# The last 96 rows of a second-layer contraction as 32-row array tiles, with five accumulation banks for that layer

One core of one Trainium2 chip (trn2). The metric is the device time of one execution in microseconds (us), the slowest core's; here there is only one core.

## The reference

Two branches over the same 2048 tokens of 512 features, mixed by a gate. Branch A is a linear attention with 32 heads; branch B is two dense layers with a ReLU between, 512 to 1376 to 512. Cut to what matters:

```python
g = sigmoid((x * gate_w).sum(-1, keepdims=True))
# A: softmax feature maps of q and k, then per head
kv  = einsum("bhsf,bhsd->bhfd", phi_k, v)
num = einsum("bhqf,bhfd->bhqd", phi_q, kv);  den = ...
a   = (num / den) @ wo
# B
h = maximum(x @ w1, 0)          # 2048 x 1376
b = h @ w2                      # contraction 1376 = 10 * 128 + 96
return g * a + (1 - g) * b
```

The second layer of B contracts over 1376 rows: ten full blocks of 128 and a rest of 96. The change is about that rest.

## The kernel before

All engines get their instructions from one plan with explicit events. The last stage (from about 87 us) works on 16 token tiles of 128 tokens. For each it runs four things: the numerators and denominators of the attention (`nd`, eight small matmuls, then a reciprocal and a product on VectorE, DVE below, then a transpose by DMA), the second layer (`finB`, eleven matmuls), the projection (`finA`, four matmuls, then a scaled copy on ScalarE, ACT below) and the combination (`comb`, one DVE instruction and the output copy).

```python
def nd(m):
    b0 = 2 * (m % 2)                                  # two pairs of PSUM banks
    ...                                               # 8 matmuls into banks b0, b0 + 1
    ...                                               # DVE: RDEN = 1/den; OTM = num * RDEN
    free[b0] = free[b0 + 1] = [f"om{m}"]
    p.dma("sp", lambda e: e.dma_start_transpose(
        out=OT[:, :, m * P:(m + 1) * P], in_=OTM[:, ob, :]), f"to{ob}", after=[f"om{m}"], ev=f"to{m}")

def finB(m, bank, cs=slice(0, 512), tag=""):
    for kt in range(KT):                              # KT = 11
        M = P if kt < KU else NR                      # the last one has NR = 96 rows
        p.op("pe", lambda e, kt=kt, M=M: e.matmul(
            PS[:, bank, 0:n], HT[0:M, kt, m * P:(m + 1) * P], W2[0:M, kt, cs],
            start=(kt == 0), stop=(kt == KT - 1)), ...)

def finA(m, bank):                                    # waits for the transpose to{m}
    for t in range(NDT):
        p.op("pe", lambda e, t=t: e.matmul(
            PS[:, bank, :], OT[:, t, m * P:(m + 1) * P], WO[:, t, :],
            start=(t == 0), stop=(t == NDT - 1)),
            after=(["wo", f"to{m}"] + free[bank] if t == 0 else ()), ...)
    ...                                               # ACT: TFA = GT * bank

FB = (4, 5, 7)                                        # banks of the second layer
for m in range(NT):
    if m > 1 and m + 3 < NT:
        nd(m + 3)                                     # three tiles ahead
    if m + 1 < NT - 1:
        finB(m + 1, FB[(m + 1) % 3])
    ...                                               # the first tiles: nd(2), nd(3), nd(4)
    finA(m, (6, 2, 0)[max(m - NT + 3, 0)])
    if m < NT - 1:
        comb(m)
...                                                   # tile 15: second layer in two cuts
```

The softmax here doesn't subtract the row's maximum and nothing guards it: scores larger than these inputs give would overflow.

Of the kernel before, what the change touches and what calls it, by code (L numbers as in the profile page):

```python
# [5 lines left out]
ACT = mybir.ActivationFunctionType  # L6
# [3 lines left out]
BF16 = mybir.dt.bfloat16  # L10
# [58 lines left out]
def bass_gated_mix__linear_kernel_hedgehog__dense_activation_relu__prompt_kernel(  # L69
# [13 lines left out]
    S, D = x2.shape  # L83
    H = A_w_phi.shape[0]
    DH = A_w_phi.shape[1]
    DFF = B_w1.shape[1]
    P = 128
    NT = S // P
    NDT = D // P
    NCH = S // 512  # L90
    KT = (DFF + P - 1) // P
# [10 lines left out]
    KU = KT - 1  # L102
    NR = DFF - KU * P

    with ExitStack() as es:
        E = es.enter_context
# [12 lines left out]
        PHQ = E(nc.sbuf_tensor("PHQ", [P, NG, S], BF16))  # L119
        KVNZ = E(nc.sbuf_tensor("KVNZ", [P, NG, 68], BF16))  # L120
        OT = E(nc.sbuf_tensor("OT", [P, NDT, S], BF16))
        HR = E(nc.sbuf_tensor("HR", [P, 2, 4, P], BF16))
        ROWI = E(nc.sbuf_tensor("ROWI", [P, P], I32))
        COLI = E(nc.sbuf_tensor("COLI", [P, P], I32))
        ONE = E(nc.sbuf_tensor("ONE", [P, 1], BF16))
# [11 lines left out]
        GT = E(nc.sbuf_tensor("GT", [P, NT], FP32))  # L137
        OMG = E(nc.sbuf_tensor("OMG", [P, NT], FP32))
        RDEN = E(nc.sbuf_tensor("RDEN", [P, 2, H], FP32))
        TFA = E(nc.sbuf_tensor("TFA", [P, 2, D], BF16))  # L140
        PS = E(nc.psum_tensor("PS", [P, 8, 512], FP32))

        XS = OT[:, 0, :].rearrange("p (j d) -> p j d", j=4)
        WQKT = PHQ[:, :, S - 512:S]
        OTM = WQK[:, 0, 0:3 * D].rearrange("p (a b) -> p a b", a=3)
        OSB = WQK[:, 1, 0:3 * D].rearrange("p (a b) -> p a b", a=3)
        EPS = 8 * 512
# [4 lines left out]
        free = {b: [] for b in range(8)}  # L152
# [126 lines left out]
        def rest(c):  # L279
            bank = nextbank()  # L280
            for i in range(4):
                for s in range(NDT):
                    t0 = c * 512 + i * P
                    p.op("pe", lambda e, i=i, s=s, t0=t0: e.matmul(  # L284
                        PS[:, bank, i * P:i * P + NR + 1], XT[:, s, t0:t0 + P], W1[:, s, KU * P:DFF + 1],
                        start=(i == 0 and s == 0), stop=(s == NDT - 1), skip_group_check=True),
                        after=(xready(c) + w1all + ["gw"] + free[bank] if i == 0 and s == 0 else ()),
                        ev=(f"h{c}_r" if i == 3 and s == NDT - 1 else None))
            src = PS[:, bank, :].rearrange("p (i n) -> p i n", i=4)
            b = c % 2  # L290
            p.op("act", lambda e: e.activation(HR[:, b, :, 0:NR], src[:, :, 0:NR], ACT.Relu),
                 after=[f"h{c}_r"] + ([f"hr{c - 2}"] if c >= 2 else []), ev=f"rr{c}")
            p.op("act", lambda e: e.activation(
                EG[:, 4 * c:4 * c + 4].unsqueeze(2), src[:, :, NR:NR + 1], ACT.Exp, scale=-1.0), ev=f"eg{c}")
            free[bank] = [f"eg{c}"]
            p.dma("sp", lambda e: e.dma_start_transpose(
                out=HT[:, KU, c * 512:(c + 1) * 512].rearrange("p (i t) -> p i t", i=4),
                in_=HR[:, b, :, :].rearrange("p i n -> p (i n)")), f"hr{c}", after=[f"rr{c}", f"hz{b}"], ev=f"hr{c}")

        def pre(i):  # L300
            which, dt = i // 4, i % 4
# [162 lines left out]
                 after=["g"], ev="gt")  # L464

        def nd(m):
            b0 = 2 * (m % 2)
            after = [f"tq{m}", "kvz0"] + free[b0] + free[b0 + 1]
            for g in range(NG):
                p.op("pe", lambda e, g=g: e.matmul(  # L470
                    PS[:, b0 + g // 4, (g % 4) * GW:(g % 4) * GW + 68],
                    PHQ[:, g, m * P:(m + 1) * P], KVNZ[:, g, :], start=True, stop=True),
                    after=(after if g == 0 else ["kvz1"] if g == 4 else ()), ev=(f"nd{m}" if g == NG - 1 else None))
            r = m % 2
            ob = m % 3
            p.op("dve", lambda e: e.reciprocal(
                RDEN[:, r, :].rearrange("p (g h) -> p g h", g=NG),
                bass.AP(tensor=PS, offset=b0 * 512 + 64, ap=[[EPS, P], [GW, NG], [1, HG]])),
                after=[f"nd{m}"], ev=f"rd{m}")
            p.op("dve", lambda e: e.tensor_tensor(  # L480
                OTM[:, ob, :].rearrange("p (g h d) -> p g h d", g=NG, h=HG),
                bass.AP(tensor=PS, offset=b0 * 512, ap=[[EPS, P], [GW, NG], [DH, HG], [1, DH]]),
                bass.AP(tensor=RDEN, offset=r * H, ap=[[2 * H, P], [HG, NG], [1, HG], [0, DH]]), ALU.mult),
                after=[f"rd{m}"] + ([f"to{m - 3}"] if m >= 3 else []), ev=f"om{m}")
# [3 lines that stand above are left out]

        fbank = {}

        def finB(m, bank, cs=slice(0, 512), tag=""):
            n = cs.stop - cs.start
            for kt in range(KT):
                M = P if kt < KU else NR
                p.op("pe", lambda e, kt=kt, M=M: e.matmul(  # L495
                    PS[:, bank, 0:n], HT[0:M, kt, m * P:(m + 1) * P], W2[0:M, kt, cs],
                    start=(kt == 0), stop=(kt == KT - 1)),
                    after=(["w2", f"hr{m // 4}", f"rl{m // 4}_{KU - 1}"] + free[bank] if kt == 0 else ()),
                    ev=(f"fb{m}{tag}" if kt == KT - 1 else None))
            fbank[(m, tag)] = bank  # L500

        def finA(m, bank):
            for t in range(NDT):
# [3 lines that stand above are left out]
                    after=(["wo", f"to{m}"] + free[bank] if t == 0 else ()),  # L507
                    ev=(f"fa{m}" if t == NDT - 1 else None))
            p.op("act", lambda e: e.activation(  # L509
                TFA[:, m % 2, :], PS[:, bank, :], ACT.Copy, scale=GT[:, m:m + 1]),  # L510
                after=[f"fa{m}", "gt"] + ([f"cb{m - 2}"] if m >= 2 else []), ev=f"ta{m}")
            free[bank] = [f"ta{m}"]
# [38 lines left out]
        slab(0)  # L551
        for b in range(VB):
            p.op("dve", lambda e, b=b: e.memset(VS[:, b, :, 64:65], 1.0), ev=f"one{b}")
        for b in range(2):
            p.op("dve", lambda e, b=b: e.memset(HR[:, b, :, NR:P], 0.0), ev=f"hz{b}")

        for b in range(NB):
            p.op("dve", lambda e, b=b: e.memset(
# [26 lines left out]
        def unit(c, k):  # L585
            if k < 0:
                rest(c)
            else:
                hunit(c, k)

        for m in range(NT):
            atile(m, None if m else 1)
            if m >= LAG:
                kv(m - LAG)
            if 0 < m < NT - 3:
                vtile(m + 3)
            for u in mid[m]:
                unit(*u)
            if m == 3:
                for a, b in ((0, 5), (5, KU)):  # L600
                    p.dma("sp", lambda e, a=a, b=b: e.dma_start(
                        out=W2[:, a:b, :], in_=B_w2[a * P:b * P, :].rearrange("(j p) n -> p j n", p=P)),
                        "w2", ev=f"w2{a}")
                p.dma("sp", lambda e: e.dma_start(out=W2[0:NR, KU, :], in_=B_w2[KU * P:DFF, :]), "w2", ev="w2")
            if m == 5:
                for a in range(0, NDT, 2):
                    p.dma("sp", lambda e, a=a: e.dma_start(
                        out=WO[:, a:a + 2, :], in_=A_wo[a * P:(a + 2) * P, :].rearrange("(j p) n -> p j n", p=P)),
                        "wo", ev="wo" if a else None)
        for i, u in enumerate(late):  # L610
            if i == 0:
                kv(NT - 3)
            if i == 2:
                kv(NT - 2)
            if i == 4:
                kv(NT - 1)
                kvfin()
            unit(*u)
        nd(0)
        qchain(NT - 1)  # L620
        gate()
        finB(0, 4)
        nd(1)
        FB = (4, 5, 7)
        for m in range(NT):
            if m > 1 and m + 3 < NT:
                nd(m + 3)
            if m + 1 < NT - 1:
                finB(m + 1, FB[(m + 1) % 3])
            if m == 1:  # L630
                nd(m + 3)
            if m == 0:
                nd(2)
                nd(3)
            finA(m, (6, 2, 0)[max(m - NT + 3, 0)])
            if m < NT - 1:
                comb(m)
        m = NT - 1
        cuts = [slice(0, 384), slice(384, 512)]
        for i, cs in enumerate(cuts):  # L640
            finB(m, (4, 3)[i], cs, "ab"[i])
        for i, cs in enumerate(cuts):
            comb(m, cs, "ab"[i], ("sp", "act")[i])
        p.wait("sp", [f"out{NT - 1}b"])
# [34 lines left out]
```

## Time and profile before

| | before |
|---|---|
| median of 6 runs (lowest, highest) | 146.75 us (146.66, 147.34) |
| profiled span | 145.1 us |
| matmul engine (PE) in the chain that ended last | 97% |
| first numerator to last combination in the chain | 87.21 to 143.57: 56.36 us |
| idle time of PE before a projection | 0.1 us in all |

The prediction below shows the lines behind this. They are read as follows: the chain of work that ended last is followed backwards, at each piece to what released it. The length of the last stage (56.36 us) is the number that I compare.

One more view of before matters later, that of the attention transposes (the last line of the view of their tile):

```profile
DMA to landing us min/median/max: 2.2/2.4/3.1
```

From issue to landing they took 2.4 us as a rule, and 3.1 once. (The view also counts two loads of the input into the same tensor, and the 2.2 is one of those; no transpose took less than 2.39 us.)

### The profile page before, as it was taken

The page shows a single profiled execution, that of the slowest core. Times are in us where ns is not written, and L with a number is a line of the kernel's source. Part 1 is how long each engine was busy: PE and PEld are TensorE (multiplying, and loading weights), DVE is VectorE, ACT ScalarE, POOL GpSimd, SP SyncE. Part 2 cuts the span into 40 slices and gives each one's busy share as a digit, 9 for nine tenths or more (in the row PEclk, how much of TensorE's full clock was granted, in tenths as well). Part 3 has the DMA queues.
Part 4 walks back from the last instruction along what each step waited for, and adds up shares of the span by engine and source line. Part 5 has one row for each costly group of instructions (what it writes and reads, how often), then busy time and mean ns, then how long its engine had stood idle before and what let it go on. Part 6 is the DMA issues. An engine that isn't in the chain of part 4 may idle for free.

```text
span 145.1 us, 2505 instructions
## 1 busy us (share of the span) xinstructions
PE 141.8 (98%) x953; PEld 72.4 (50%) x970; DVE 92.3 (64%) x157; ACT 72.1 (50%) x125; POOL 52.1 (36%) x62
## 2 busy tenths in 40 slices
PE   8999999999999999999999999999999999999994
PEld 3444654444455555644655545554444544444443
DVE  4338557977686788678698968664555555545342
ACT  4134677778878778788878861122111111111150
POOL 2031002977878668668879801200000000000000
DMA  5999985042369974315334332355332223322213
GB/s 157 268 287 202 242 177 113 3 99 47 72 142 349 143 171 107 71 29 111 77 72 107 74 72 41 83 106 132 80 75 72 72 72 75 75 72 75 72 45 106
DMA packets 46517, 16.12 MB, mean 111 GB/s; under 512 B 40392, under 2 KB 46120, under 8 KB 46504
## 3 DMA queue, kind: packets, MB, share of 16 engines
q1 hardware_dynamic: 46352, 15.92, 48.9%
q8 instruction: 8, 0.13, 0.4%
q14 instruction: 5, 0.04, 0.1%
q10 hardware_dynamic: 152, 0.03, 0.1%
HBM read 4.15 MB, written 2.10 MB: 43 GB/s over the span
## 4 chain that ended last, share of the span: by engine, by line
PE 97%; issue 1%; DVE 1%; DVEq 0%
PE PS L495 26%; PE PS L272 19%; PE PS L351 18%; PE PS L504 9%; PE PS L416 9%; PE PS L532 5%; PE PS L470 3%; PE PS L438 3%; PE PS L284 2%; PE PS L231 2%; PE PS L306 1%; DVE WQK L518 1%; PE PS L237 1%; DVE ONE L207 0%; DVEq L664 0%
## 5 line engine op out<-in xcount | busy, mean ns | idle before, releaser
L495 PE MATMUL PS<-W,HT 128*128 128x512 bf16 (+3 forms) x182 | 40.2, 366 | 0.3
L384 POOL TENSOR_TENSOR EB<-EB,SC 128x1024 bf16<-128x1024 bf16 x15 | 28.9, 1928 | 23.2 <-DVE SC L382 23.2
L335 ACT ACTIVATE EB<-PS 128x480 bf16<-128x480 f32 (+1 forms) x46 | 30.4, 732 | 13.4 <-PE PS L351 13.4
L509 ACT ACTIVATE TFA<-PS,GT 128x512 bf16<-128x512 f32 x16 | 11.0, 687 | 42.7 <-PE PS L504 42.7
L272 PE MATMUL PS<-XT,W 128*128 128x512 bf16 x122 | 30.1, 379 | 0.4
L351 PE MATMUL PS<-WQK,XT 128*128 128x480 bf16 x128 | 28.7, 366 | 0.0
L518 DVE SCALAR_TENSOR_TENSOR WQK<-PS,OMG,TFA 128x512 bf16<-128x512 f32 (+2 forms) x17 | 12.2, 719 | 23.6 <-ACT TFA L509 22.4
L495 PEld LDWEIGHTS PS<-W,HT 128*128 128x128 bf16 (+1 forms) x187 | 17.1, 98 | 17.4
L380 DVE TENSOR_REDUCE ZB<-EB 128x64 f32<-128x1024 bf16 x15 | 18.3, 1220 | 11.4 <-ACT EB L335 11.4
L258 ACT ACTIVATE HT<-PS 128x512 bf16<-128x512 f32 x34 | 19.8, 615 | 7.5 <-PE PS L532 5.9
L351 PEld LDWEIGHTS PS<-WQK,XT 128*128 128x128 bf16 x128 | 12.4, 98 | 13.7 <-DVE WQK L311 0.3
L395 DVE TENSOR_REDUCE ZB<-EB 128x64 f32<-128x1024 bf16 x16 | 18.6, 1164 | 0.0
L272 PEld LDWEIGHTS PS<-XT,W 128*128 128x128 bf16 x128 | 11.9, 98 | 13.0
L404 POOL TENSOR_TENSOR EB<-EB,SC 128x512 bf16<-128x512 bf16 x16 | 16.9, 1056 | 1.3
L504 PE MATMUL PS<-WO,OT 128*128 128x512 bf16 x62 | 16.0, 378 | 0.1
L416 PE MATMUL PS<-WV,XT 128*128 128x512 bf16 x60 | 15.5, 378 | 0.2
L480 DVE TENSOR_TENSOR WQK<-PS,RDEN 128x512 bf16<-128x512 f32 x16 | 11.1, 691 | 0.5
L426 ACT ACTIVATE VS<-PS 128x512 bf16<-128x512 f32 x14 | 8.5, 610 | 2.3 <-PE PS L416 2.3
L504 PEld LDWEIGHTS PS<-WO,OT 128*128 128x128 bf16 x64 | 6.1, 97 | 7.2
L382 DVE RECIPROCAL SC<-ZB 128x64 f32<-128x64 f32 x16 | 8.8, 553 | 0.5
L416 PEld LDWEIGHTS PS<-WV,XT 128*128 128x128 bf16 x64 | 5.4, 97 | 5.0 <-DVE VS L424 0.4
L470 PEld LDWEIGHTS PS<-KVNZ,PHQ 128*128 128x128 bf16 x128 | 6.1, 97 | 3.6
(57 smaller groups left out, 86.5 us busy)
## 6 DMA issues: line engine op xcount, KB each, us to landing
out_dram<-WQK SPq DMA_DIRECT2D x15, 128.0 KB, 1.7
W<-in_B_w_dram SPq DMA_DIRECT2D x2, 640.0 KB, 5.3
W<-in_B_w_dram SPq DMA_DIRECT2D x3, 256.0 KB, 3.2
WV<-in_A_wqkv_dram SPq DMA_DIRECT2D x1, 512.0 KB, 5.3
WO<-in_A_wo_dram SPq DMA_DIRECT2D x2, 256.0 KB, 3.0
W<-in_B_w_dram SPq DMA_DIRECT2D x1, 352.0 KB, 4.3
OT<-in_A_x_dram SPq DMA_DIRECT2D x2, 128.0 KB, 2.2
W<-in_B_w_dram SPq DMA_DIRECT2D x2, 128.0 KB, 2.3
```

The costliest lines, as they stand in the source:

```text
L258: p.op("act", lambda e: e.activation(dst, src, ACT.Relu), after=[f"h{c}_{kt}"], ev=ev)
L272: p.op("pe", lambda e, t=t: e.matmul(PS[:, bank, :], W1[:, t, kt * P:(kt + 1) * P], XT[:, t, c * 512:(c + 1) * 512], start=(t == 0), stop= ...
L335: p.op("act", lambda e: e.activation(dst, s_, ACT.Exp, scale=scale), after=[qk] + busy, ev=ev)
L351: p.op("pe", lambda e, dt=dt, which=which: e.matmul(PS[:, which, 0:DE], XT[:, dt, m * P:(m + 1) * P], WQK[:, which, dt * DE:(dt + 1) * DE] ...
L380: p.op("dve", lambda e: e.tensor_reduce(zk, ek, AX.X, ALU.add), after=[emk, f"cst{b}"], ev=f"zk{m}")
L384: p.op("pool" if m < NT - 1 else "dve", lambda e: e.tensor_tensor(EB[:, b, 3, :].rearrange("p (g f) -> p g f", f=DH), EB[:, b, 2, :].rearr ...
L395: p.op("dve", lambda e: e.tensor_reduce(ZB[:, b, 0:64].rearrange("p (h s) -> p h s", s=2), bass.AP(tensor=EB, offset=base, ap=[[EBS, P], [ ...
L404: p.op("pool", lambda e: e.tensor_tensor(EB[:, b, 0, :].rearrange("p (h s f) -> p h s f", h=H, s=2)[:, :, 1, :], EB[:, b, 1, :].rearrange( ...
L416: p.op("pe", lambda e, dt=dt: e.matmul(PS[:, bank, :], XT[:, dt, m * P:(m + 1) * P], WV[:, dt, :], start=(dt == 0), stop=(dt == NDT - 1)), ...
L495: p.op("pe", lambda e, kt=kt, M=M: e.matmul(PS[:, bank, 0:n], HT[0:M, kt, m * P:(m + 1) * P], W2[0:M, kt, cs], start=(kt == 0), stop=(kt = ...
L504: p.op("pe", lambda e, t=t: e.matmul(PS[:, bank, :], OT[:, t, m * P:(m + 1) * P], WO[:, t, :], start=(t == 0), stop=(t == NDT - 1)), after ...
L518: p.op("dve", lambda e: e.scalar_tensor_tensor(out=OSB[:, ob, cs], in0=PS[:, bank, 0:n], scalar=OMG[:, m:m + 1], in1=TFA[:, m % 2, cs], op ...
```

## The change

A matmul with 96 rows takes as long as one with 128 (381 and 379 ns in the lines of the prediction). The intent is to do the rest of four token tiles at once: the 96 rows are cut into three blocks of 32, and four of the 32-row matmuls (a wave, one for each token tile) are meant to run side by side. Three such waves replace four 96-row matmuls. For this the hidden values are transposed into another layout, the last 96 rows of the weight are copied into each of the four row groups (W2R), and the change gives each of the four tiles a bank of its own. Token tiles 0 to 11 are done so, in three chunks ("packs"); tiles 12 to 15 stay as before. By a change of mode I mean no more than the step from full matmuls to 32-row ones or back.

```diff
+        W2R = E(nc.sbuf_tensor("W2R", [P, 3, D], BF16))
...
-        TFA = E(nc.sbuf_tensor("TFA", [P, 2, D], BF16))
+        TFA = WQK[:, :, 3 * D:4 * D]
... (relu of the rest: three blocks of 32 rows for four token tiles)
         def nd(m):
-            b0 = 2 * (m % 2)
+            b0 = 0
...
-        def finB(m, bank, cs=slice(0, 512), tag=""):
+        def finB(m, bank, cs=slice(0, 512), tag="", mid=None):
...
+            packed = m < NT - 4
+            kts = range(KU) if packed else range(KT)
... (a packed tile: ten matmuls that add to what the pack began)
+        def packs(c, banks):
+            for k in range(3):
+                for i in range(4):
+                    t0 = c * 512 + k * P
+                    p.op("pe", lambda e, i=i, k=k, t0=t0: e.matmul(
+                        PS[:, banks[i], :], HT[32 * i:32 * i + 32, KU, t0:t0 + P], W2R[32 * i:32 * i + 32, k, :],
+                        start=(k == 0), stop=False, skip_group_check=True),
+                        after=(["w2", f"hr{c}"] + free[banks[i]] if k == 0 else ()))
... (the weight loads: one copy in place of two, three more for W2R)
+        FB = (2, 7, two, 6, one)
...
-        for m in range(NT):
-            if m > 1 and m + 3 < NT:
-                nd(m + 3)
-            if m + 1 < NT - 1:
-                finB(m + 1, FB[(m + 1) % 3])
...
+        for m in range(NT - 1):
+            if m % 4 == 0 and m < NT - 4:
+                packs(m // 4, [fb(m + i) for i in range(4)])
+                if m:
+                    nd(m + 1)
+            mid3 = None
+            if m == 3:
+                def mid3():
+                    finA(2, last)
+                    comb(2)
+            finB(m, fb(m), mid=mid3)
+            if m < 4:
+                nd(m + 1)
+            elif m + 2 < NT and m + 2 != 9:
+                nd(m + 2)
+            if 1 <= m < 3:
+                finA(m - 1, last)
+                comb(m - 1)
+            if m >= 3:
+                finA(m, last)
+                comb(m)
+        finA(NT - 1, 0)
```

With one pair of banks for the numerators instead of two, the order had to be rewritten.

More of the change, by code (lines that the diff above doesn't have):

```diff
@@ L121, in bass_gated_mix__linear_kernel_hedgehog__dense_activation_relu__prompt_kernel @@
         OT = E(nc.sbuf_tensor("OT", [P, NDT, S], BF16))
-        HR = E(nc.sbuf_tensor("HR", [P, 2, 4, P], BF16))
+        HR = E(nc.sbuf_tensor("HR", [P, 1, 3, P], BF16))
+        HR3 = E(nc.sbuf_tensor("HR3", [P, 4, P], BF16))
+        W2R = E(nc.sbuf_tensor("W2R", [P, 3, D], BF16))
         ROWI = E(nc.sbuf_tensor("ROWI", [P, P], I32))
@@ L289, in rest @@
             src = PS[:, bank, :].rearrange("p (i n) -> p i n", i=4)
-            b = c % 2
-            p.op("act", lambda e: e.activation(HR[:, b, :, 0:NR], src[:, :, 0:NR], ACT.Relu),
-                 after=[f"h{c}_r"] + ([f"hr{c - 2}"] if c >= 2 else []), ev=f"rr{c}")
+            b = 0
+            if c < NCH - 1:
+                p.op("act", lambda e: e.activation(
+                    HR[:, b, :, :].rearrange("p r (i n) -> p i r n", i=4),
+                    src[:, :, 0:NR].rearrange("p i (r n) -> p i r n", r=3), ACT.Relu),
+                    after=[f"h{c}_r"] + ([f"hr{c - 1}"] if c else []), ev=f"rr{c}")
+            else:
+                p.op("act", lambda e: e.activation(HR3[:, :, 0:NR], src[:, :, 0:NR], ACT.Relu),
+                     after=[f"h{c}_r"], ev=f"rr{c}")
             p.op("act", lambda e: e.activation(
@@ L295, in rest @@
             free[bank] = [f"eg{c}"]
-            p.dma("sp", lambda e: e.dma_start_transpose(
-                out=HT[:, KU, c * 512:(c + 1) * 512].rearrange("p (i t) -> p i t", i=4),
-                in_=HR[:, b, :, :].rearrange("p i n -> p (i n)")), f"hr{c}", after=[f"rr{c}", f"hz{b}"], ev=f"hr{c}")
+            if c < NCH - 1:
+                p.dma("sp", lambda e: e.dma_start_transpose(
+                    out=HT[:, KU, c * 512:c * 512 + 384].rearrange("p (r t) -> p r t", r=3),
+                    in_=HR[:, b, :, :].rearrange("p r n -> p (r n)")), f"hr{c}", after=[f"rr{c}"], ev=f"hr{c}")
+            else:
+                p.dma("sp", lambda e: e.dma_start_transpose(
+                    out=HT[:, KU, c * 512:(c + 1) * 512].rearrange("p (i t) -> p i t", i=4),
+                    in_=HR3[:, :, :].rearrange("p i n -> p (i n)")), f"hr{c}", after=[f"rr{c}", "hz"], ev=f"hr{c}")
         def pre(i):
@@ L489, in bass_gated_mix__linear_kernel_hedgehog__dense_activation_relu__prompt_kernel @@
         fbank = {}
-        def finB(m, bank, cs=slice(0, 512), tag=""):
+        def finB(m, bank, cs=slice(0, 512), tag="", mid=None):
             n = cs.stop - cs.start
-            for kt in range(KT):
+            packed = m < NT - 4
+            kts = range(KU) if packed else range(KT)
+            for kt in kts:
+                if mid is not None and kt == KU // 2:
+                    mid()
                 M = P if kt < KU else NR
@@ L496, in finB @@
                     PS[:, bank, 0:n], HT[0:M, kt, m * P:(m + 1) * P], W2[0:M, kt, cs],
-                    start=(kt == 0), stop=(kt == KT - 1)),
-                    after=(["w2", f"hr{m // 4}", f"rl{m // 4}_{KU - 1}"] + free[bank] if kt == 0 else ()),
-                    ev=(f"fb{m}{tag}" if kt == KT - 1 else None))
+                    start=(kt == 0 and not packed), stop=(kt == kts[-1]), skip_group_check=packed),
+                    after=(["w2", f"rl{m // 4}_{KU - 1}"] + ([] if packed else [f"hr{m // 4}"] + free[bank])
+                           if kt == 0 else ()),
+                    ev=(f"fb{m}{tag}" if kt == kts[-1] else None))
             fbank[(m, tag)] = bank
+        def packs(c, banks):
[6 more added lines that the diff above has]
+                        after=(["w2", f"hr{c}"] + free[banks[i]] if k == 0 else ()))
         def finA(m, bank):
@@ L553, in bass_gated_mix__linear_kernel_hedgehog__dense_activation_relu__prompt_kernel @@
             p.op("dve", lambda e, b=b: e.memset(VS[:, b, :, 64:65], 1.0), ev=f"one{b}")
-        for b in range(2):
-            p.op("dve", lambda e, b=b: e.memset(HR[:, b, :, NR:P], 0.0), ev=f"hz{b}")
+        p.op("dve", lambda e: e.memset(HR3[:, :, NR:P], 0.0), ev="hz")
         for b in range(NB):
@@ L599, in bass_gated_mix__linear_kernel_hedgehog__dense_activation_relu__prompt_kernel @@
             if m == 3:
-                for a, b in ((0, 5), (5, KU)):
+                for a, b in ((0, KU),):
                     p.dma("sp", lambda e, a=a, b=b: e.dma_start(
@@ L603, in bass_gated_mix__linear_kernel_hedgehog__dense_activation_relu__prompt_kernel @@
                         "w2", ev=f"w2{a}")
-                p.dma("sp", lambda e: e.dma_start(out=W2[0:NR, KU, :], in_=B_w2[KU * P:DFF, :]), "w2", ev="w2")
+                p.dma("sp", lambda e: e.dma_start(out=W2[0:NR, KU, :], in_=B_w2[KU * P:DFF, :]), "w2", ev="w2n")
+                for k in range(3):
+                    p.dma("sp", lambda e, k=k: e.dma_start(
+                        out=W2R[:, k, :],
+                        in_=bass.AP(tensor=B_w2.tensor, offset=(KU * P + 32 * k) * D, ap=[[0, 4], [D, 32], [1, D]])),
+                        "w2", ev=f"w2r{k}" if k < 2 else "w2")
             if m == 5:
-                for a in range(0, NDT, 2):
+                for a in range(0, NDT, NDT):
                     p.dma("sp", lambda e, a=a: e.dma_start(
-                        out=WO[:, a:a + 2, :], in_=A_wo[a * P:(a + 2) * P, :].rearrange("(j p) n -> p j n", p=P)),
-                        "wo", ev="wo" if a else None)
+                        out=WO[:, a:a + NDT, :], in_=A_wo[a * P:(a + NDT) * P, :].rearrange("(j p) n -> p j n", p=P)),
+                        "wo", ev="wo")
         for i, u in enumerate(late):
@@ L618, in bass_gated_mix__linear_kernel_hedgehog__dense_activation_relu__prompt_kernel, with fb @@
             unit(*u)
+        last = 3 + (rot[0] - 1) % 3
+        one, two = 3 + (rot[0] - 2) % 3, 3 + (rot[0] - 3) % 3
+        FB = (2, 7, two, 6, one)
+        def fb(m):
+            return FB[m % 5]
         nd(0)
@@ L621, in bass_gated_mix__linear_kernel_hedgehog__dense_activation_relu__prompt_kernel @@
         gate()
-        finB(0, 4)
-        nd(1)
-        FB = (4, 5, 7)
-        for m in range(NT):
-            if m > 1 and m + 3 < NT:
-                nd(m + 3)
-            if m + 1 < NT - 1:
-                finB(m + 1, FB[(m + 1) % 3])
-            if m == 1:
-                nd(m + 3)
-            if m == 0:
-                nd(2)
-                nd(3)
-            finA(m, (6, 2, 0)[max(m - NT + 3, 0)])
-            if m < NT - 1:
+        for m in range(NT - 1):
[18 more added lines that the diff above has]
+                finA(m, last)
                 comb(m)
+        finA(NT - 1, 0)
         m = NT - 1
@@ L640, in bass_gated_mix__linear_kernel_hedgehog__dense_activation_relu__prompt_kernel @@
         for i, cs in enumerate(cuts):
-            finB(m, (4, 3)[i], cs, "ab"[i])
+            finB(m, (fb(m), fb(m + 1))[i], cs, "ab"[i])
         for i, cs in enumerate(cuts):
```

## The prediction

> **What bounds the kernel now.** I read the page first: engine totals, slices, and the chain of work that ended last.
>
> ```profile
> span 145.1 us, 2505 instructions
> ...
> PE 141.8 (98%) x953; PEld 72.4 (50%) x970; DVE 92.3 (64%) x157; ACT 72.1 (50%) x125; POOL 52.1 (36%) x62
> ...
> PE   8999999999999999999999999999999999999994
> ...
> PE 97%; issue 1%; DVE 1%; DVEq 0%
> ```
>
> The matmul engine (PE) is busy in every slice. Its busy time alone proves little, because the records of pipelined matmuls overlap each other; the last line is the proof: 97% of the chain that sets the end is PE's own work, and the other engines hold 1%. Nothing that only relieves another engine or a DMA can shorten this kernel much.
>
> Next I followed the chain in order of time through the last stage (87 us to the end), which the change rewrites. Columns are start, length, engine, tile and line, count:
>
> ```profile
> 115.08 2.38 PE PS L495 x11
> 117.45 0.86 PE PS L504 x4
> 118.32 0.26 PE PS L470 x8
> 118.57 1.73 PE PS L495 x8
> 120.30 0.05 issue
> 120.35 0.60 PE PS L495 x2
> ```
>
> L495 is the second layer, L504 the output projection of the attention side, L470 its numerator and denominator. A token tile (128 tokens) takes 2.38 + 0.86 + 0.26 = 3.50 us, and the next starts at once: 115.08 to 118.57. A matmul 512 columns wide therefore costs 2.38 / 11 = 0.216 us of PE's time; the pieces called issue (0.05 us, about every 7.8 us) are the only holes.
>
> Last, the groups with shapes kept apart:
>
> ```profile
> L495 PE MATMUL PS<-W,HT 128*128 128x512 bf16 x145 | 34.4, 379 | 0.3
> ...
> L495 PE MATMUL PS<-W,HT 96*128 96x512 bf16 x15 | 5.7, 381 | 0.0
> ```
>
> The last columns of a group are busy time, mean ns of one, and idle time before it. The 379 and 381 ns are latencies of one matmul, 0.216 us is its share of a stream. So a matmul with 96 rows costs the same 0.216 us as one with 128[...]. And the eight pairs of weight load and 68-column matmul at 118.32 above pass at 0.26 / 8 = 32 ns each, which bounds how fast PE can be given work.
>
> [...] The trace before has no change of mode; I must guess this cost, and the whole answer depends on it. [...] The change gives each of the four its own bank, which is why it needs five second-layer banks.
>
> **The change, part by part.**
>
> Removed: the eleventh matmul (96 rows) of token tiles 0 to 11: 12 x 0.216 = 2.59 us, all on the path.
>
> Added: three packs, each 12 matmuls of 32 rows, in three waves of four token tiles. If the four of a wave overlap wholly, a wave costs one stream time, a pack 3 x 0.216 = 0.65 us and three packs 1.94 us. So the most that can be won is 2.59 - 1.94 = 0.65 us, or 0.4% of the time. [...]
>
> Against it stand two costs per pack. First the start: four load-and-matmul pairs at 32 ns put the fourth tile some 3 x 32 = 0.1 us behind the first; later waves keep that distance, it is paid once: 0.3 us in all. [...] Second the change of mode, in and out, six in all. An upper estimate for one is the part of a matmul's latency that a stream hides, 0.379 - 0.216 = 0.16 us; at half of that, 0.08 us, six cost 0.5 us. Sum of the hopeful case (full overlap, start hidden by weights loaded early, 0.04 us per change of mode): -0.65 + 0.24 = -0.4 us. Middle case (start of 0.1 us, 0.08 us per change): -0.65 + 0.3 + 0.5 = +0.15 us. [...]
>
> Moved: with five banks for the second layer, one for the projection and two for the numerator, the last two lose their double buffers. I checked the new order for each wait against durations of the trace. Numerator: after its matmuls come a reciprocal (0.35 us) and a product (0.69 us), some 1.1 us before the two banks are free; the closest two are those around the second pack, with a projection (0.86) and a pack (at least 0.65) between them, 1.5 us. Projection: ACT empties its bank in 0.69 us; the closest two are tiles 2 and 3, with five matmuls (1.08) and a numerator (0.26) between, 1.34 us. Second pack: its fourth bank is freed by the combination of tile 2, which ends 0.69 + 0.75 us plus small gaps, about 1.5 us, after that tile's projection; the pack starts 1.08 + 0.26 + 0.86 = 2.2 us after it. The attention transposes land 2.4 us after their issue and have four to five microseconds. None of these waits should appear.
>
> Loads: three copies of the last 96 rows of the second weight, spread over the four row groups, add 384 KB near 42 us. 640 KB landed in 5.3 us there, so I expect one to three microseconds more of the queue. The phi transposes behind them have five buffers, over 15 us of slack. The second-layer weights are needed only at 87 us. The transposes of the 96 rows shrink from four blocks to three. ACT's relu writes the same 384 elements per partition (0.51 us before), only in another order. All this lies beside PE's work and should give nothing.
>
> **Rivals.** (1) The four row tiles don't overlap at all. Then the packs cost 36 x 0.216 = 7.8 us against 2.59 removed: +5.2 us, about 152.0. For it: nothing in the trace shows overlap. [...] (3) A single-buffered bank stalls PE: at most a few tenths per occurrence, since the smallest margin above is 0.4 us; if it came at every tile, 15 x 0.2 = 3 us, 149.8. The durations speak against it. (4) The win is the full 0.65 us: 146.2.
>
> **Range and chances.** The bound of -0.65 us makes a gain of 2% (2.9 us) impossible unless something outside the reckoning happens; I leave 1%. The hopeful and middle cases together give about -0.1 us; that this is a reworked order, tuned to hide its own waits, makes me lean slightly to the hopeful one. Prediction 146.7 us; the range 146.1 (full win) to 147.8 (bad case). Slower by over 2% needs rival 1 or 3: 6%.
>
> **What would show it.** In the changed profile: 15 - 12 = 3 matmuls left with 96 rows and 512 columns; 36 with 32 rows; a chain still near 97% PE. A pack in the chain in order of time should take 0.7 to 1.0 us including both changes of mode; 0.86 is break-even, and 2.6 would be rival 1. A token tile without its eleventh matmul should take 2.16 + 0.86 + 0.26 = 3.28 us. PE waiting for the numerator's product, for ACT's scaled copy or for a combination would show rival 3. I am wrong if a pack lies outside 0.65 to 1.15 us, if holes open in PE during the stage before 87 us, or if the last tile's end (two cuts, unchanged) takes another length.

## The result, and the profile after

| | before | changed |
|---|---|---|
| median of 6 runs (lowest, highest) | 146.75 (146.66, 147.34) | 148.66 (148.03, 150.11) |
| profiled span | 145.1 | 148.8 |
| first numerator to last combination | 56.36 | 58.75 |
| idle time of PE before a projection | 0.1 | 2.2 |

The ratio is 1.0136 (95% interval 1.0088 to 1.0183): slower by 1.4%, still inside 2%, but outside the range that I gave (its upper end, the 147.8 us of a bad case, was my estimate; no trace showed it). Ratios here and below are the mean time of one kernel's fast runs over that of the other's of the same rounds, so they are not quite the ratios of the medians. The profiled run was the slowest of the six: its last stage began at 88.49 us, 1.28 us later than before, with the same work for PE up to there. A second profile of the changed kernel (below) began it at 87.41, so this part is the scatter of the start and not the change.

The page of the changed kernel, engine totals, PE's slices and the chain:

```profile
span 148.8 us, 2549 instructions
...
PE 143.3 (96%) x977; PEld 71.8 (48%) x994; DVE 93.3 (63%) x156; ACT 72.1 (48%) x125; POOL 52.1 (35%) x62
...
PE   8999999999999999999999999999799999999964
...
PE 89%; DMA 7%; DVE 1%; issue 1%; SPq 0%; ACT 0%
```

PE's share of the chain has fallen from 97% to 89%, and DMA, which had no part in it, holds 7%. There are two dents in PE's slices: a 7 in the 29th and a 6 near the end. The chain in order of time, at a pack and at the two dents (L524 is the pack, L512 the second layer, L483 the numerator, L531 the projection):

```profile
88.49 0.25 PE PS L483 x8
88.75 0.76 PE PS L524 x12
89.51 1.83 PE PS L512 x8
...
103.05 3.93 DMA OT<-WQK
106.98 0.04 issue
107.02 1.04 PE PS L531 x4
...
117.63 0.76 PE PS L524 x12
118.39 0.36 PE PS L483 x8
...
137.73 0.27 PE PS L483 x8
138.00 0.03 issue
138.03 0.37 DVE RDEN L489
138.40 0.02 issue
138.42 0.70 DVE WQK L493
139.12 0.02 issue
139.14 4.22 DMA OT<-WQK
143.36 0.05 issue
143.41 1.04 PE PS L531 x4
```

Two things are to be read here. First the packs: twelve matmuls in 0.76 us. Then the work after a pack is 0.10 us longer than elsewhere: eight matmuls in 1.83 us where 8 x 0.216 = 1.73, and a numerator in 0.36 instead of 0.26. A pack thus costs 0.86 us, against 4 x 0.216 = 0.864 us for the matmuls that it replaces. Second the holes: the chain leaves PE, goes through the attention transpose (OT<-WQK) of tile 4 at 103.05 and of tile 15 at 139.14, and comes back with the projection. The waits, columns being waiter, cause, us in total, times, longest:

```profile
PE PS L531 <- DMA OT<-WQK: 2.1, 2, 1.3
```

And the landing times of these transposes:

```profile
DMA to landing us min/median/max: 2.3/2.4/4.2
```

PE idled 0.78 and 1.31 us in the two holes, and the first four matmuls after each took 1.04 us instead of 0.86: 0.18 us more each. I call this refilling; it is close to 0.379 - 0.216 = 0.16 us, the difference between one matmul's latency and its share of a stream. Holes 2.09 + refilling 0.36 - packs 3 x 0.004 = 2.4 us, and the stage is 58.75 - 56.36 = 2.39 us longer. So the account closes to 0.05 us.

Why did two of sixteen transposes take about 4 us, when the median stayed at 2.4? In the trace the semaphore of each transpose gets sixteen increments; I take them as one from each of the core's 16 DMA engines. For tile 15, fifteen of the sixteen had come at 141.6 us, in good time for the projection, which PE could have started at 142.1; the sixteenth came at 143.4. In between, the DMA view for 141 to 142 us shows

```profile
q8 instruction: 1, 0.02, 5.9%
q14 instruction: 1, 0.01, 3.6%
```

The columns are packets, MB and share of 16 engines' time. One packet of 16 KB with instructions took 5.9% of 16 engines for 1 us, which is one engine for 0.95 us. At tile 4 a packet of 16 KB began at 104.1 and took 1.47 us, just when that transpose was moving: all but 33 of its 512 data packets had started by 105.0, the last 33, about a sixteenth of them, ran singly from 105.6, when the fetch ended, to 106.4, and all sixteen increments came together at 106.9 to 107.0. So at tile 15 one increment came late, and at tile 4 all sixteen.

This holds beyond these two. The fourteen profiles of this study contain 224 of these transposes. In 37 of them, those that took more than 2.6 us (4.5 at the most), a 16 KB fetch was under way or began between issue and landing; the other 187 took 2.39 to 2.51 us, and no such fetch began during any of them.

Hence **theory A**: the new order left some 4.1 us (tile 15; 4.4 at tile 4) between the end of a numerator on PE and its projection. DVE takes 1.1 us of it and the transpose 2.4, so about 0.5 us is left; if a fetch of instructions then holds up one of the sixteen engines, the projection waits for that one. The packs themselves win nothing and cost nothing. The rivals: **B**, the packs, their changes of mode or the added loads cost the time, and the holes would only move; **C**, the transposes land late in this order whatever the fetch does, because output copies are ahead of them in the queue.

### The profile page after: what moved, and what is told of

Same layout as the page of the kernel before. It is cut to its first block, busy times and chain, and to the rows that moved or that the text cites. A ratio compares the mean times of both kernels' runs of the same rounds, so it can differ in the third digit from the quotient of the medians.

```text
span 148.8 us, 2549 instructions
## 1 busy us (share of the span) xinstructions
PE 143.3 (96%) x977; PEld 71.8 (48%) x994; DVE 93.3 (63%) x156; ACT 72.1 (48%) x125; POOL 52.1 (35%) x62
## 4 chain that ended last, share of the span: by engine, by line
PE 89%; DMA 7%; DVE 1%; issue 1%; SPq 0%; ACT 0%
PE PS L512 20%; PE PS L274 18%; PE PS L364 17%; PE PS L429 9%; PE PS L531 8%; PE PS L559 6%; DMA OT<-WQK 5%; PE PS L451 3%; PE PS L483 2%; PE PS L286 2%; DMA OT<-in_A_x_dram 2%; PE PS L319 1%; PE PS L524 1%; DVE WQK L545 1%; DVE WQK L493 0%
## 5 line engine op out<-in xcount | busy, mean ns | idle before, releaser
L512 PE MATMUL PS<-W,HT 128*128 128x512 bf16 (+3 forms) x170 | 37.6, 366 | 0.3
L536 ACT ACTIVATE WQK<-PS,GT 128x512 bf16<-128x512 f32 x16 | 11.0, 687 | 45.0 <-PE PS L531 45.0
L274 PE MATMUL PS<-XT,W 128*128 128x512 bf16 x122 | 30.1, 379 | 0.3
L512 PEld LDWEIGHTS PS<-W,HT 128*128 128x128 bf16 (+1 forms) x175 | 16.5, 98 | 18.5 <-issue 0.4
L545 DVE SCALAR_TENSOR_TENSOR WQK<-PS,OMG,WQK 128x512 bf16<-128x512 f32 (+2 forms) x17 | 12.2, 719 | 15.6 <-ACT WQK L536 13.0
L531 PE MATMUL PS<-WO,OT 128*128 128x512 bf16 x62 | 16.0, 379 | 2.2 <-DMA OT<-WQK 2.1
L489 DVE RECIPROCAL RDEN<-PS 128x32 f32<-128x32 f32 x16 | 5.7, 356 | 12.6 <-PE PS L483 12.6
L531 PEld LDWEIGHTS PS<-WO,OT 128*128 128x128 bf16 x64 | 5.3, 97 | 7.2 <-DMA OT<-WQK 2.7
L559 PE MATMUL PS<-XT,W 128*128 128x512 bf16 x32 | 8.4, 428 | 0.0
```

The lines of the kernel that those rows point to most:

```text
L274: p.op("pe", lambda e, t=t: e.matmul(PS[:, bank, :], W1[:, t, kt * P:(kt + 1) * P], XT[:, t, c * 512:(c + 1) * 512], start=(t == 0), stop= ...
L512: p.op("pe", lambda e, kt=kt, M=M: e.matmul(PS[:, bank, 0:n], HT[0:M, kt, m * P:(m + 1) * P], W2[0:M, kt, cs], start=(kt == 0 and not pack ...
L531: p.op("pe", lambda e, t=t: e.matmul(PS[:, bank, :], OT[:, t, m * P:(m + 1) * P], WO[:, t, :], start=(t == 0), stop=(t == NDT - 1)), after ...
L559: p.op("pe", lambda e, u=u: e.matmul(PS[:, UB[u], :], W1[:, t, u * P:(u + 1) * P], XT[:, t, 0:512], start=(t == 0), stop=(t == NDT - 1)), ...
```

## The experiments

Twelve runs were made, of ten new kernels (e11_tail_again and e12_after_again repeat e2_tail and the changed kernel); each has runs of the kernel before on the same chip. All gave right results.

### Numerators earlier, both places: e1_both

```diff
 (pack)     if m:
-                    nd(m + 1)
+                    nd(m + 1 if m == 4 else m + 2)
 (mid3)  def mid3():
+                    nd(4)
                     finA(2, last)
...
-            if m < 4:
+            if m < 3:
                 nd(m + 1)
-            elif m + 2 < NT and m + 2 != 9:
+            elif 3 < m < 8:
                 nd(m + 2)
+            elif 8 <= m and m + 3 < NT:
+                nd(m + 3)
```

> The changed kernel with the numerator of tile 4 computed 2.2 us earlier (in the middle of the second layer of tile 3) and those of tiles 9 to 15 one tile earlier, so that the transposes of tiles 4 and 15 get over 6 us from the numerator to the projection instead of about 4.1. Theory A (the two holes of the matmul engine, 0.93 us before the projection of tile 4 and 1.48 us before that of tile 15, each with some 0.18 us of refilling, are the whole loss, and the packs win 0.10 us each): no wait on the transposes is left, and the time is the time before less 0.3: 146.3 to 146.6. Theory B (the packs, the changes of mode or the added loads cost the time, the holes only shift it): 148 or more. Theory C (see e4_fetch) says the same as A here.

Measured: 147.03 us (before 146.93), ratio 1.0002 (0.997 to 1.0033). No wait on a transpose is left, although two transposes still met a fetch and took 3.9 and 4.1 us: with the longer lead they were in time. The stage took 56.32 us. That decides against B. The size is off by 0.3 us: I had still counted a win of 0.10 us for a pack, from its 0.76 us alone, and had overlooked the 0.10 us after it. (The expectation also put the two holes a little too long, at 0.93 and 1.48 us; the profile says 0.78 and 1.31.)

### Only one of the two places: e2_tail, e3_head, e11_tail_again

e2_tail has only the edit of the numerators 9 to 15, e3_head only `nd(4)` in `mid3`.

> Only the numerators of tiles 9 to 15 moved earlier; tile 4 left as in the changed kernel. Theory A: the hole before the projection of tile 15 goes (1.5 to 1.7 us), the one before tile 4 stays where the instruction fetch still meets it: 146.6 to 147.4. Theory B: 148 or more.

Measured: 147.01 us, ratio 0.9999 (0.9968 to 1.003). I had expected the hole at tile 4 to stay. It did not come: the transpose of tile 4 landed at 104.4 us, and the fetch that had met it at 104.1 came at 107.3 (the last stage of this profile began 1.09 us earlier). The chain at the end shows PE without a hole (second layer of tile 14, projections of 14 and 15, the two cuts of 15):

```profile
136.81 2.38 PE PS L512 x11
139.19 1.73 PE PS L531 x8
140.92 1.80 PE PS L512 x11
```

> Only the numerator of tile 4 moved earlier; tile 15 left. Theory A: the hole before tile 4 goes (about 1 us), the one before tile 15 stays: 147.2 to 147.9. Theory B: 148 or more.

Measured: 148.47 us, ratio 1.0104 (1.0072 to 1.0135), outside what I expected and inside what theory B says: removing the hole at tile 4 gained nothing. But its profile shows the loss in holes again: the one at tile 15 stayed (1.2 us), and a small new one (0.1 us) opened at tile 9, whose transpose met a fetch and took 4.3 us. So tile 15 is the usual loss; the first hole comes at tile 4 or tile 9, wherever the fetch falls.

> e2_tail once more, unchanged, on the same chip as e9_nopack2 for a direct comparison: within 0.2 us of the kernel before.

Measured: 146.97 us, ratio 0.9994 (0.9974 to 1.0013). It was run at another time. Both results of this version equal the kernel before.

### Moving the fetch, with the order untouched: e4_fetch and its control e10_control

```diff
-        warm(4)
+        warm(20, 102)        # e4_fetch;   e10_control: warm(6, 341)
```

The aim was to bring the fetch to another time, with nearly the same columns in the warm-up (2048 before, 2040 and 2046 here): its four matmuls become twenty in e4_fetch and six in e10_control. That the number of PE's instructions sets when the fetch comes was my guess.

> The changed kernel with its order untouched; only the four 512-column warm-up matmuls at the start are cut into twenty of 102 columns, the same work, 16 weight loads and 16 matmuls more. [...] Theory A with its trigger (the fetch, on one of the 16 DMA engines, holds up one sixteenth of the transpose: in the changed kernel's trace 15 of the 16 increments of tile 15 had come at 141.52, before the projection needed them at 141.93, and the last at 143.29): both holes shrink below 0.3 us and the time is 146.4 to 147.0. Theory C (the transposes land late in this order whatever the fetch does, because output copies are ahead of them in the queue): unchanged, 148 to 149.

Measured: 146.91 us, ratio 0.9996 (0.9965 to 1.0028). No hole was left, with the numerators as late as in the changed kernel. The fetch came at 136.4 us, before the transpose of tile 15 was issued (137.86), and all sixteen increments were in at 140.3. It fell on the transpose of tile 14 instead, which took 4.0 us and had the time. C falls: the output copies ahead in the queue are the same. (The 141.52, 141.93 and 143.29 of the expectation are slightly early; the trace has 141.59, 142.10 and 143.36.)

> The control for e4_fetch: the changed kernel with its warm-up cut as well, but into six matmuls of 341 columns, only 4 instructions of the matmul engine more. [...] Theory A with its trigger: 148.0 to 148.9 as the changed kernel. If it was the cutting of the warm-up that had helped in e4_fetch: 147.

Measured: 148.56 us, ratio 1.0099 (1.0079 to 1.012). So it was not the cutting of the warm-up. The profile has only the hole at tile 15:

```profile
136.33 0.27 PE PS L483 x8
136.60 0.02 issue
136.62 0.37 DVE RDEN L489
136.99 0.02 issue
137.01 0.70 DVE WQK L493
137.72 0.02 issue
137.73 3.89 DMA OT<-WQK
141.62 0.05 issue
141.67 1.04 PE PS L531 x4
```

One idle time of 1.0 us and 0.18 of refilling: the stage is 57.48 us, 1.12 longer than before. The fetch near tile 4 came at 108.0 this time, though the program there is that of the changed kernel but for four instructions; so the count of instructions alone doesn't place it.

### The changed kernel: e12_after_again

> The changed kernel again, unchanged, for a second profile. The one so far was its slowest run (150.11 us), with a slow start and two holes; e10_control, all but the same program, had only the hole at tile 15, 148.3 to 148.75. If the hole at tile 15 is the usual loss and the one at tile 4 an occasional one: 148.0 to 148.9 us and a hole at tile 15 of 1 to 1.6 us. If both are usual: both holes, 149 or more.

Measured: 148.75 and 148.03 us (before 146.72). The profile has a hole at tile 15 of 1.5 us and a small one of about 0.3 us at tile 9, none at tile 4. So neither of the two expectations is quite met, and what e3_head said is confirmed. Together, for tile 15 (times in us of each profile, to about 0.1, from the increments and packets of the trace):

```
kernel            issued  16 KB fetch  15th of 16  16th    PE idle
changed           139.1   141.4        141.6       143.4   1.3
e12_after_again   137.6   140.0        140.0       142.0   1.5
e3_head           137.3   139.4        139.8       141.4   1.2
e10_control       137.7   139.5        140.1       141.6   1.0
e4_fetch          137.9   136.4        140.3       140.3   none
```

In all five the fifteenth increment comes 2.4 to 2.5 us after the issue. Where a fetch begins about 2 us after the issue, the sixteenth is 1.5 to 2.0 us later. That is more than the 0.9 to 1.05 us that the packet itself took. In all four the last packets of the output copy that was issued after the transpose ran singly until some 0.7 us after the fetch, and the sixteenth increment came 0.3 to 0.5 us after those; whether it had to wait for them too is not shown.

### What a pack costs: e5_nopack, e9_nopack2, e6_split

e5_nopack is e2_tail with the 96-row matmul back in each tile (`packed = False`, no call of `packs`, the old layout for the hidden values).

> The version with the early tail (e2_tail: its order, its banks, its loads), but without packs: the last 96 rows again as the eleventh matmul of each token tile. Theory D (from the traces: a pack takes 0.76 us and the first matmuls after it 0.10 us more, 0.86 us in all, just what the four matmuls cost that it replaces): same time as e2_tail within 0.2 us, stage from the first numerator to the end 56.3 to 56.5 us in the trace. If the packs had won their full 0.65 us, it would be 0.65 us slower; if they had cost something, faster.

Measured: 148.56 us, ratio 1.0112 (1.008 to 1.0145). This is no answer to the question, as its chain shows:

```profile
101.15 0.27 PE PS L483 x8
101.42 0.02 issue
101.44 0.37 DVE RDEN L489
101.81 0.02 issue
101.83 0.70 DVE WQK L493
```

With the pack gone, two numerators stood only a projection (0.86 us) apart, and the second waited for DVE to free their one pair of banks, twice. My kernel was badly made; it shows what the pack's place is worth as a spacer. e9_nopack2 moves the second numerator into the middle of the second layer:

```diff
-                if m:
-                    nd(m + 1 if m == 4 else m + 2)
             mid3 = None
+            if m in (4, 8):
+                def mid3(m=m):
+                    nd(m + 1 if m == 4 else m + 2)
```

> e5_nopack mended: there two numerators followed each other with only a projection between, because the pack that had spaced them was gone, and the matmul engine waited for the two banks twice. Here the second of them stands in the middle of the second layer's matmuls. Theory D (a pack is worth what it replaces): no hole, stage from first numerator to end 56.3 to 56.5 us, time within 0.2 us of e11_tail_again. If packs had won their full 0.65 us: 0.65 us slower than it.

Measured: 147.69 us (146.54 to 148.29), ratio 1.0031 (0.9999 to 1.0064), against 146.97 for e11_tail_again. The difference of 0.7 us can't be read as the packs' win: in the profiled run, the slowest of the six, PE idled 1.8 us once at 21 us, in the start of the kernel that scatters from run to run, long before the packs; the other five runs have no profile. The stage took 56.70 us against 56.32; twice the bank of the numerators still came 0.17 us late. Taking these two off, 56.36 is left, 0.04 us over the version with packs. The trace says break-even; the timed runs alone would not decide it.

e6_split is e2_tail with the three waves of each pack apart:

```diff
+                if packed and m % 4 == 0 and kt in (3, 6):
+                    packs(m // 4, [fb(m + i) for i in range(4)], (kt // 3,))
...
-                packs(m // 4, [fb(m + i) for i in range(4)])
+                packs(m // 4, [fb(m + i) for i in range(4)], (0,))
```

> e2_tail with the three waves of each pack apart: one before, one after three and one after six of the ten full matmuls of the first token tile. Same matmuls, six more visits to the 32-row mode. Theory D (entering costs about 0.11 us with the start of the first wave, leaving 0.10 us, a wave in the stream 0.216): 6 x 0.21 = 1.3 us slower than e2_tail. Rival E (the change of mode is free, and waves are slow, 0.287 us each): same as e2_tail.

Measured: 148.83 us, ratio 1.0117 (1.0089 to 1.0146), while e2_tail had 0.9999. The chain at the first pack (L526 is a wave, L514 the second layer):

```profile
87.56 0.33 PE PS L526 x4
87.89 0.75 PE PS L514 x3
88.64 0.33 PE PS L526 x4
88.97 0.75 PE PS L514 x3
89.72 0.33 PE PS L526 x4
90.05 0.97 PE PS L514 x4
```

A wave alone takes 0.33 us, and the three full matmuls after it 0.75 instead of 0.65. So a visit to the 32-row mode costs 0.33 - 0.216 = 0.11 us to enter, start of the first wave included, and 0.10 us to leave. Three waves in one visit take 0.76 = 0.11 + 3 x 0.216: within a visit the four tiles overlap fully. Six more visits make 1.3 us; the stage is 57.92 - 56.32 = 1.60 us longer, and the rest fits two numerators that here waited for their banks, at 102.29 and 117.13 us. Rival E, slow waves, falls. By an estimate that takes 0.216 us for a 32-row matmul by itself (no run has one), a visit of one wave does its work 4 x 0.216 / (0.33 + 0.10) = 2.0 times as fast as one matmul after another, and a visit of three waves 12 x 0.216 / (0.76 + 0.10) = 3.0 times.

### The short lead in the kernel before: e7_late, e8_late_fetch

```diff
-            if m > 1 and m + 3 < NT:
+            if m > 1 and m + 3 < NT - 1:
                 nd(m + 3)
+            if m == NT - 3:
+                nd(NT - 1)
```

e8_late_fetch has `warm(16, 128)` in place of `warm(4)` as well, meant to bring the fetch onto the transpose of tile 15, by the same guess.

> The kernel before, with only the numerator of tile 15 computed one tile later, at the distance that it has in the changed kernel (a numerator to projection distance of 4.1 us). No packs, no added loads, four second-layer banks as before. The fetch of the matmul engine was at 140.8 there, after the transpose should have landed (about 139.2), so theory A expects no hole or less than 0.3 us: 146.8 to 147.1. If the short lead alone were enough, some 1.5 us slower.

> e7_late with the warm-up cut into sixteen of 128 columns, 24 matmul-engine instructions more[...]. Theory A: a hole of 0.6 to 1.3 us before the last projection, 147.5 to 148.4. If the fetch has nothing to do with it: same as e7_late.

Measured: 148.13 us, ratio 1.0064 (1.0038 to 1.009), and 148.30 us, ratio 1.0085 (1.0062 to 1.0108). The expectation for e7_late failed: there was a hole, and 1.0 us was lost. In its chain:

```profile
136.40 0.70 ACT TFA L509
...
137.17 0.09 DVE WQK L518
...
137.84 0.36 DVE RDEN L476
138.20 0.02 issue
138.22 0.70 DVE WQK L480
138.93 0.02 issue
138.94 2.42 DMA OT<-WQK
141.37 0.05 issue
141.41 1.04 PE PS L504 x4
```

The transpose took an ordinary 2.42 us. But the numerator stood behind a combination in DVE's queue, and that waited for ACT; DVE came to the reciprocal only 1.2 us after the end of the numerator (0.04 us in the changed kernel). The distance on PE was the 4.1 us of the changed kernel, the lead of the transpose was not. PE idled 0.7 us, the stage took 57.23 us. In e8_late_fetch the fetch did not move onto the transpose (142.8 us, 142.4 in e7_late), so it is the same experiment again. Its time and its hole of 0.7 us lie in the range that I had named for theory A, but by luck: it tests nothing of the fetch. What both do show: in the kernel before, without packs and with its two pairs of numerator banks, this one late numerator costs 0.9 us of the stage (57.23 - 56.36), all by itself.

## Why the prediction was wrong

- **Limit of the win (0.65 us) and the middle case (+0.15 us): right in mechanism, nearly right in size.** Full overlap within a wave is measured (0.216 us a wave). I had put the start at 0.10 us and a change of mode at 0.08, together 0.26 us a visit; entering with the start takes 0.11 us and leaving 0.10, together 0.21. So a pack costs 0.86 us, which the prediction had named as break-even. Three packs make -0.01 us, and the stage of e1_both and e2_tail is 0.04 us shorter than before.
- **Rivals 1 and 4** did not come: no missing overlap and no full win. Nor did the changes of mode cost more than the waves win (0.21 us a pack against 0.864 - 0.648 = 0.216). (Rival 4 has a slip: 146.75 - 0.65 is 146.1, as in the range, and not 146.2.)
- **Banks (rival 3):** no numerator, projection or pack of the changed kernel waits for a bank. The margins reckoned there were right; e5_nopack, which takes a pack from between two numerators, shows how narrow that margin is.
- **The step that failed** is in the part on what moved: "The attention transposes land 2.4 us after their issue and have four to five microseconds. None of these waits should appear." The four microseconds were counted from the numerator on PE (4.1 at tile 15), not from the issue. 1.1 us of them belong to DVE, and 3.0 are left for the transpose. And 2.4 us was a median; the four transposes of tile 15 in the table above that met a fetch of instructions took 3.9 to 4.4 us. The landing view of before would have shown a maximum of 3.1; I had not asked for it. The wait cost 1.1 to 2.4 us of the stage in three profiles of the changed kernel and its control. Of the signs that the prediction listed, the chain is the one that showed it (near 97% PE expected, 89% found).
- **Early loads and the stage before 87 us:** as predicted, nothing. The second profile of the changed kernel began the last stage at 87.41 us, before 87.21. And in e7_late and e8_late_fetch, which have the loads of the kernel before, it began at 88.02 and 88.05, so a late start needs no added loads.
- **The range** was skewed to the wrong side because I had put only PE's costs into its upper end, no DMA wait.

What is shown: the holes are the loss (e1_both, e2_tail, e11_tail_again), and whether the hole at tile 15 opens hangs on when the fetch comes (e4_fetch against e10_control, the table of five profiles, and the count over 224 transposes). What is only argued: that each of the sixteen increments stands for one DMA engine, and that it is PE's instructions that are fetched. For the second speaks that only PE's program differs in e4_fetch, where the fetch came at 136.4 us and not at 141.4; the views show the packets as "instruction", but not for which engine. What stays open: what sets the moment of a fetch. In e10_control and e8_late_fetch it did not follow the count of instructions. Open, too, is the part of the delay beyond the packet's own time.

No version beat the kernel before. The best, e2_tail, equals it: what the packs save is spent on changing the mode.

## What to carry to other kernels

In this kernel a packed matmul had to save more than the visit to its mode cost (0.21 us, about one stream slot of 512 columns at 0.216): three waves in place of four slots just paid for it, so by this sum longer visits are wanted or none (no run has a longer one). When an order is rewritten to free buffers, reckon each transfer's lead from the end of its last producer on every engine between, each in its queue's order, and set the slowest landing against it (here 4.2 us), not the median (2.4). The matmul engine of the kernel before waited only 0.1 us before its projections; in the new order a sixteenth increment that was 1.5 to 2.0 us late left it idle for 1.0 to 1.5 us before the projection of tile 15.
